# Batch 0's v loads on another engine's queue, and a planner that models GpSimd's load queue

## The chip, the cores and the metric

The kernel runs on one core of a Trainium2 chip. The metric is device time in microseconds (us). A core has five engines that each work through their own instructions in order: TensorE (PE in the profile), VectorE (DVE), ScalarE (ACT), GpSimd (POOL) and SyncE (SP). SP, ACT and POOL can also issue loads and stores, which 16 DMA engines carry out.

## The reference

Attention with a bias by distance, in 8 batches of 8 heads, 576 tokens, 64 channels a head, and behind it a feed-forward layer with a leaky ReLU over all 4608 tokens:

```python
scores = q @ k.T / sqrt(64)
scores = scores + bias_table[bucket(|i - j|)]      # 32 buckets, the last from distance 128 on
attn = softmax(scores)
x = (attn @ v) as [4608, 512]
h = x @ w_in                                       # w_in [512, 2048]
y = max(0.01 * h, h) @ w_out                       # w_out [2048, 512]
```

All inputs and the output are float32; the kernel multiplies in bf16.

## The kernel before

The work of attention is cut into 32 pairs of heads, numbered 0 to 31: four pairs a batch, so pairs 0 to 3 are batch 0, 4 to 7 batch 1, and 8 is the first of batch 2. For a pair, VectorE copies the q and k rows (`rows`, L383), TensorE turns them (`turn_by_pe`, L393), the turned q and k go to `qt` and `kt` (L405), and `apart` (L409) makes the copies for the odd last 64 tokens. TensorE computes the scores in six units u0 to u5 (`score`, L430 to L438), ScalarE takes the exponential of each (`expo`, L444 to L451), VectorE multiplies in the bias near the diagonal (`band`, L463), TensorE multiplies with v in two halves (`av`, L478 and L480), VectorE normalises (L489, L490), and the result is turned into `xT` (L504, L508, or by a DMA). For batch 0 the second half of `av` has a buffer of its own, called ps_om. Scores of pair n are kept in one of two buffers; pair 2 has a third one, and pair 3 writes the buffer that pair 0 used.

The bias enters as a factor: the table's exponential (`exp_table`, L296) is spread by one matmul to a row u (L300, L303), stored to DRAM (`store_u_row`, L306) and read back as band tables hk and hk4 (`load_hk`, L316, and `load_hk4`, L323), all on SP's queue.

The feed-forward layer works on tiles of 512 tokens: 16 blocks of `ffn_in` (4 matmuls each, L521) with a ReLU on ScalarE (L526), then `ffn_out` (L533), a copy (L538) and a store (L543). The first tile lies within batch 0 and needs both halves of w_in, of which blocks 0 to 7 need the first; `ffn_out` needs w_out.

Loads: q and k of the first pair come by SP and ACT. v of batch 0 comes in float32 by six DMAs (`load_v_raw`, L310 and L312, 1.18 MB) and GpSimd casts it (`cast_v`, L331 and L334). All other loads are issued by GpSimd, which casts them on the way, in one queue. Batch b's rows of q and k are in qn0, kn0 for even b and qn1, kn1 for odd b. A `gate` (L337) is a one-element copy on GpSimd into w_in's tile: it waits for its source, and the load of w_in that writes the same bytes waits for it.

The order of the instructions on every engine is set when the kernel is built. `Plan` holds tasks with an engine, a cost in us, the tasks that they come after, and a rank. `Plan.order` simulates the engines and takes, again and again, the task that can start first; the instructions are then written in that order. The costs are thus guesses that decide the order, and the chip then runs each engine's list in order, whatever the true times are. Where the planner expects TensorE to idle, before the first feed-forward block, it puts filler matmuls (`spin`, L710). For a load, `tail` and `land` say when the planner believes that its data is there.

## Time and profile before

| | us |
|---|---|
| median of 3 runs (405.65 to 408.68) | 407.63 |
| the profiled execution | 407.88 |
| its span, first to last instruction | 406.1 |
| TensorE busy | 377.5 (93%) |
| ScalarE busy | 243.2 (60%) |
| VectorE busy | 203.8 (50%) |
| GpSimd busy | 69.8 (17%) |
| mean granted TensorE clock | 0.971 of 2.4 GHz |

The span is what the trace covers; the timed value is 1.8 us longer. A busy time says what share of the span an engine computed, not whether it set the end: matmuls overlap, and an engine that is busy 60% of the time can still be what another waits for in some stretch. The mean clock lies under 1, so part of the execution ran at the lower level of 1.2 GHz.

### The profile page before, as it was taken

The page shows a single profiled execution, that of the slowest core. Times are in us where ns is not written, and L with a number is a line of the kernel's source. Part 1 is how long each engine was busy: PE and PEld are TensorE (multiplying, and loading weights), DVE is VectorE, ACT ScalarE, POOL GpSimd, SP SyncE. Part 2 cuts the span into 40 slices and gives each one's busy share as a digit, 9 for nine tenths or more (in the row PEclk, how much of TensorE's full clock was granted, in tenths as well). Part 3 has the DMA queues.
Part 4 walks back from the last instruction along what each step waited for, and adds up shares of the span by engine and source line. Part 5 has one row for each costly group of instructions (what it writes and reads, how often), then busy time and mean ns, then how long its engine had stood idle before and what let it go on. Part 6 is the DMA issues. An engine that isn't in the chain of part 4 may idle for free.

```text
span 406.1 us, 8302 instructions
## 1 busy us (share of the span) xinstructions
PE 377.5 (93%) x3388; PEld 191.5 (47%) x3388; DVE 203.8 (50%) x539; ACT 243.2 (60%) x345; POOL 69.8 (17%) x112
## 2 busy tenths in 40 slices
PE   3898906999999999999999999999999999999995
PEld 1355403555454554545555455555555544444442
DVE  3498305887667767668567555555444210101021
ACT  1696912856897697877777777777777233333300
POOL 5492613101500700420160040000000000000000
PEclk8699975999999999999999999999999999999999
DMA  9759999833995994898399399111111010010112
GB/s 182 171 84 203 181 205 156 108 87 84 130 154 114 121 184 76 104 178 131 84 149 186 80 105 90 44 44 44 43 44 44 27 46 31 32 47 26 53 52 77
DMA packets 102741, 40.62 MB, mean 100 GB/s; under 512 B 81704, under 2 KB 97072, under 8 KB 102704
## 3 DMA queue, kind: packets, MB, share of 16 engines
q0 software_dynamic: 48512, 17.47, 39.8%
q1 hardware_dynamic: 49280, 21.15, 25.8%
q10 hardware_dynamic: 4912, 1.48, 1.8%
q8 instruction: 26, 0.43, 0.4%
q14 instruction: 11, 0.09, 0.1%
HBM read 37.69 MB, written 9.45 MB: 116 GB/s over the span
## 4 chain that ended last, share of the span: by engine, by line
PE 84%; DMA 9%; ACTq 2%; POOL 2%; issue 1%; DVE 1%; ACT 1%; POOLq 0%
PE pm L533 31%; PE pm L521 30%; PE ps_o L478 9%; PE ps_s L430 7%; DMA kn<-in_k_dram 4%; DMA v<-in_v_dram 4%; PE ps_o L480 2%; DMA w_in_sb<-in_moe_w_in_dram 2%; PE ps_s L434 1%; PE ps_s L437 1%; ACTq L312 1%; PE ps_t L393 1%; POOL vn L331 1%; ACTq L310 1%; PE ps_w L710 0%
## 5 line engine op out<-in xcount | busy, mean ns | idle before, releaser
L521 PE MATMUL pm<-xT,w_in_sb 128*128 128x512 bf16 x576 | 147.2, 383 | 0.0
L533 PE MATMUL pm<-w_out_sb,gt 128*128 128x512 bf16 x576 | 144.3, 379 | 0.0
L526 ACT ACTIVATE gt<-pm 128x512 bf16<-128x512 f32 x144 | 86.1, 601 | 92.2 <-PE pm L521 90.9
L444 ACT ACTIVATE at<-ps_s 128x1024 bf16<-128x1024 f32 x124 | 120.1, 1024 | 27.0 <-PE ps_s L430 26.4
L533 PEld LDWEIGHTS <-gt 128*128 128x128 bf16 x576 | 52.6, 98 | 67.1 <-issue 10.6
L521 PEld LDWEIGHTS <-w_in_sb 128*128 128x128 bf16 x576 | 52.8, 98 | 63.5 <-issue 6.8
L463 DVE TENSOR_TENSOR at<-at,hk 128x768 bf16<-128x768 bf16 (+3 forms) x155 | 69.4, 461 | 22.1 <-ACT at L444 17.2
L478 PEld LDWEIGHTS <-at 128*128 128x128 bf16 x1240 | 52.7, 98 | 31.0 <-DVE at L463 16.7
L538 DVE COPY y<-pm 128x512 f32<-128x512 f32 x36 | 24.8, 690 | 83.8 <-PE pm L533 83.4
L478 PE MATMUL ps_o<-vn,at 128*128 128x65 bf16 x1180 | 54.0, 195 | 13.6 <-DVE at L463 13.6
L480 PE MATMUL ps_o<-v,at 128*128 128x65 bf16 x295 | 47.9, 195 | 0.2 <-POOL v L334 0.2
L201 POOL DMA_DIRECT2D vn<-in_v_dram x24 | 21.6, 911 | 141.4 <-PE ps_o L480 132.3
L430 PE MATMUL ps_s<-qt,kt 64*128 64x512 bf16 x256 | 40.9, 388 | 1.2 <-ACT at L446 0.5
L489 DVE RECIPROCAL rcp<-ps_o 128x5 f32<-128x5 f32 x60 | 11.7, 194 | 43.5 <-PE ps_o L480 43.1
L490 DVE TENSOR_TENSOR opair<-ps_o,rcp 128x320 bf16<-128x320 f32 x60 | 29.5, 492 | 2.0
L480 PEld LDWEIGHTS <-at 128*128 128x128 bf16 x310 | 30.4, 98 | 0.0
L446 ACT ACTIVATE at<-ps_s 128x512 bf16<-128x512 f32 x31 | 18.6, 601 | 11.4 <-PE ps_s L434 11.3
L405 DVE COPY qt<-tu 128x576 bf16<-128x576 bf16 x22 | 14.8, 670 | 14.1 <-PE ps_s L438 14.1
L451 ACT ACTIVATE at<-ps_s 128x576 bf16<-128x576 f32 x31 | 20.3, 655 | 0.2 <-PE ps_s L438 0.2
L383 DVE COPY pr<-qn 96x768 bf16<-96x768 bf16 x31 | 11.1, 358 | 15.2 <-DMA qn<-in_q_dram 15.2
L430 PEld LDWEIGHTS <-kt 64*128 64x128 bf16 x256 | 8.5, 94 | 21.5 <-issue 18.7
L405 DVE COPY kt<-tu 128x576 bf16<-128x576 bf16 x22 | 14.7, 667 | 0.0
(77 smaller groups left out, 202.2 us busy)
## 6 DMA issues: line engine op xcount, KB each, us to landing
out_dram<-y SPq DMA_DIRECT2D x36, 256.0 KB, 2.0
qn<-in_q_dram POOLq DMA_DIRECT2D x14, 288.0 KB, 9.9
kn<-in_k_dram POOLq DMA_DIRECT2D x14, 288.0 KB, 10.7
vn<-in_v_dram POOLq DMA_DIRECT2D x28, 128.0 KB, 6.0
w_in_sb<-in_moe_w_in_dram POOLq DMA_DIRECT2D x2, 1024.0 KB, 11.6
w_out_sb<-in_moe_w_out_dram POOLq DMA_DIRECT2D x2, 1024.0 KB, 13.9
first<-in_v_dram ACTq DMA_DIRECT2D x4, 256.0 KB, 8.7
hk<-u_row SPq DMA_DIRECT2D x1, 576.0 KB, 6.2
```

The costliest lines, as they stand in the source:

```text
L201: nc.gpsimd.dma_start(out=vn[i][:, c, :, 0:D], in_=v[b, :, c * P : (c + 1) * P, :].rearrange("h s d -> s h d"),)
L405: copy(out=t[:, 0:S].rearrange("p (r c) -> p r c", c=NC), in_=src)
L430: nc.tensor.matmul(ps[:, e, :], lhsT=kt[r, u * P : (u + 1) * P], rhs=qt[r, 0:512], start=True, stop=True)
L444: nc.scalar.activation(at[:, :, u, 0:512], ps, AF.Exp, scale=scale)
L463: nc.vector.tensor_tensor(out=o, in0=o, in1=m, op=ALU.mult)
L478: nc.tensor.matmul(ps[:, ic, :], lhsT=at[:, o : o + P], rhs=vn[i][:, c, 2 * p + e, :], start=(c == 0), stop=False)
L480: nc.tensor.matmul(ps[:, ic, :], lhsT=at4[:, ic * P : (ic + 1) * P], rhs=v4[i][:, p, e, :], start=False, stop=True)
L490: nc.vector.tensor_tensor(out=opairs[n][:, :, e * D : (e + 1) * D], in0=ps[:, :, 0:D], in1=rcp.to_broadcast([P, NJ + 1, D]), op=ALU.mult)
L521: nc.tensor.matmul(pm[:, j * w : (j + 1) * w], lhsT=w_in_sb[:, c, f * P : (f + 1) * P], rhs=xT[c][:, t0 : t0 + w], start=(c == 0), stop=(c ...
L526: nc.scalar.activation(gts[T][:, f0 : f0 + TT // w, 0:w], pms.pop((T, f0)).rearrange("p (j t) -> p j t", t=w), AF.Prelu, bias=0.0, scale=1 ...
L533: nc.tensor.matmul(ys[T, ts], lhsT=gts[T][:, f, ts * P : (ts + 1) * P], rhs=w_out_sb[:, f, :], start=(f == 0), stop=(f == n_fc - 1))
L538: nc.vector.tensor_copy(out=y, in_=ys[T, ts])
```

## The change

It does four things. The six v loads of batch 0 are issued by SP, as a task that comes after the store of the u row, and whose rank puts it behind the band loads. The planner gets a model of GpSimd's load queue: each load has a time `moves`, and `ring` makes each load's data come after that of the load before; the numbers for `land` and `tail` go. The gate of w_in's first half waits for the last v load in place of hk, and the casts of v stand behind that load's issue. And v of batch 1 is loaded before the second half of w_in. Some costs and due times are set anew.

```diff
@@ -59,7 +59,7 @@
 
     def order(self):
 
-        free, done, waiting = {}, [], {}
+        free, done, waiting, ring = {}, [], {}, 0.0
         for t in self.tasks:
             waiting.setdefault(t["engine"], []).append(t)
         first = False
@@ -90,7 +90,9 @@
             _, t, r = best
             e = t["engine"]
             waiting[e].remove(t)
-            t["start"], t["end"] = r, max(r + t["cost"] + t["tail"], t.get("land", 0.0))
+            t["start"], t["end"] = r, r + t["cost"] + t["tail"]
+            if "moves" in t:
+                t["end"] = ring = max(ring, r + t["cost"] + 2.0) + t["moves"]
             t["idle"] = r - free.get(e, 0.0)
             free[e] = r + t["cost"]
             for k in t["take"]:
@@ -307,9 +309,9 @@
 
     def load_v_raw():
         for c in range(NJ):
-            nc.scalar.dma_start(out=vraw_sb[:, c, :, :], in_=v[0, :, c * P : (c + 1) * P, :].rearrange("h s d -> s h d"))
+            nc.sync.dma_start(out=vraw_sb[:, c, :, :], in_=v[0, :, c * P : (c + 1) * P, :].rearrange("h s d -> s h d"))
         for e in range(2):
-            nc.scalar.dma_start(out=vraw4[e * SL : (e + 1) * SL, :, :],
+            nc.sync.dma_start(out=vraw4[e * SL : (e + 1) * SL, :, :],
                                 in_=v[0, e::2, NJ * P : S, :].rearrange("h s d -> s h d"))
 
     def load_hk(h0, h1):
@@ -333,8 +335,8 @@
         for e in range(2):
             nc.gpsimd.tensor_copy(out=v4[0][e * SL : (e + 1) * SL, :, e, 0:D], in_=vraw4[e * SL : (e + 1) * SL, :, :])
 
-    def gate(t):
-        nc.gpsimd.tensor_copy(out=w_in_sb[0:1, 0, 0:1], in_=t)
+    def gate(t, row=0):
+        nc.gpsimd.tensor_copy(out=w_in_sb[row : row + 1, 0, 0:1], in_=t)
 
     def mirrored(t, lo, hi):
 
@@ -550,37 +552,39 @@
     def dma(at):
         return add("DMA0", 0.0, [], None, 0, at=at)
 
-    L["raw", 0], L["raw", 1], tabl = dma(3.6), dma(3.8), dma(3.4)
+    L["raw", 0], L["raw", 1], tabl = dma(4.0), dma(4.2), dma(3.8)
     sh = add("DVE", 0.1, [tabl], shift_table, -1)
     e8t = add("ACT", 0.25, [sh], exp_table, -1)
     spr = add("PE", 0.4, [e8t], spread_table, -1, take=["O"])
     cpu = add("DVE", 0.6, [spr], copy_u_row, -1, give=["O"])
-    urt = add("SP", 0.1, [cpu], store_u_row, -1, tail=2.6)
-    hkt = add("SP", 0.1, [urt], lambda: load_hk(0, 2), -1, tail=2.8)
+    urt = add("SP", 0.1, [cpu], store_u_row, -1, tail=2.8)
+    hkt = add("SP", 0.1, [urt], lambda: load_hk(0, 2), -1, tail=3.2)
     hkr = add("SP", 0.1, [urt], lambda: (load_hk(2, H), load_hk4()), 1, tail=5.5)
+    vrt = add("SP", 0.5, [urt], load_v_raw, 2, tail=6.0)
+    vrt["land"] = 18.0
     L["hk", 0], L["hk", 1] = hkt, hkr
 
     prev = []
 
-    def pool_load(key, cost, go, after=(), land=0.0):
-        t = add("POOL", cost, prev + list(after), go, 1, tail=2.5)
-        t["land"] = land
+    def pool_load(key, cost, go, moves, after=(), rank=1):
+        t = add("POOL", cost, prev + list(after), go, rank)
+        t["moves"] = moves
         prev[:] = [t]
         L[key] = t
-
+        return t
+
+    QK, VB, WH = 3.9, 9.5, 5.6
     L["qk", 0, 0], L["qk", 0, 1] = dma(7.0), dma(9.5)
-    pool_load(("qk", 0, 2), 1.6, lambda: (gate(ub[0:1, 0:1]), load_qk(0, 6, H)), after=[cpu], land=17.0)
-    vrt = add("ACT", 0.6, [], load_v_raw, 5, tail=9.0)
-    vc = [add("POOL", 0.7, [vrt], lambda c=c: cast_v(c), 0) for c in range(NJ + 1)]
+    pool_load(("qk", 0, 2), 1.6, lambda: (gate(ub[0:1, 0:1]), load_qk(0, 6, H)), QK / 2, after=[cpu])
+    pool_load(("w_in", 0), 1.0, lambda: (gate(vraw4[SL : SL + 1, 0, 0:1], SL), load_w_in(0)), WH, after=[vrt])
+    vc = [add("POOL", 0.6, [vrt] + prev, lambda c=c: cast_v(c), 0) for c in range(NJ + 1)]
     vt[0] = vc[-1]
-    pool_load(("w_in", 0), 0.8, lambda: (gate(hk[0:1, H - 1, 0:1]), load_w_in(0)), after=[hkr], land=22.0)
-    pool_load(("qk", 1, 0), 1.6, lambda: load_qk(1, 0, 4), land=26.0)
-    pool_load(("w_in", 1), 0.8, lambda: load_w_in(1), land=32.0)
-    pool_load(("v", 1), 5.5, lambda: load_v(1, 0, H, False), land=42.0)
-    vt[1] = L["v", 1]
-    pool_load(("qk", 1, 1), 1.6, lambda: load_qk(1, 4, H), land=46.0)
-    pool_load(("w_out", 0), 0.9, lambda: load_w_out(0), land=52.0)
-    pool_load(("w_out", 1), 0.9, lambda: load_w_out(1), land=58.0)
+    pool_load(("qk", 1, 0), 1.6, lambda: load_qk(1, 0, 4), QK)
+    vt[1] = pool_load(("v", 1), 5.5, lambda: load_v(1, 0, H, False), VB)
+    pool_load(("w_in", 1), 0.8, lambda: load_w_in(1), WH)
+    pool_load(("qk", 1, 1), 1.6, lambda: load_qk(1, 4, H), QK)
+    pool_load(("w_out", 0), 0.9, lambda: load_w_out(0), WH)
+    pool_load(("w_out", 1), 0.9, lambda: load_w_out(1), WH)
 
     def plan_rows(n):
         b, p = items[n]
...
@@ -667,11 +671,9 @@
         i = n_pairs * (b - 2)
         for hh in range(2):
             ps = [rowt[i + 2 * hh + x][r] for x in range(2) for r in range(2)]
-            L["qk", b, hh] = add("POOL", 1.5, ps + prev, lambda hh=hh: load_qk(b, 4 * hh, 4 * hh + 4), 10 * i + 500, tail=11.0)
-            prev[:] = [L["qk", b, hh]]
+            pool_load(("qk", b, hh), 1.5, lambda hh=hh: load_qk(b, 4 * hh, 4 * hh + 4), QK, ps, 10 * i + 500)
         avs = [t for p in range(n_pairs) for t in avt[i + p]]
-        vt[b] = add("POOL", 5.0, avs + prev, lambda: [load_v_part(b, j) for j in range(3)], 10 * i + 500, tail=11.0)
-        prev[:] = [vt[b]]
+        vt[b] = pool_load(("v", b), 5.0, lambda: [load_v_part(b, j) for j in range(3)], VB, avs, 10 * i + 500)
 
     yts, oin, ins = [], {}, {}
 
```

On ScalarE, from its start: `e_171` is the exponential of the bias table, `first` the tile that receives raw q, k and v. Before:

```order
L256 DMA first<-in_k_dram 96x2x384
L261 ACT_TABLE_LOAD
L261 ACTIVATE warm<-warm 128x1
L310 DMA first<-in_v_dram 128x8x64 x4
L312 DMA first<-in_v_dram 64x4x64 x2
L296 ACTIVATE e_171<-tab 32x8
L383 CAST pr<-first 96x768
L405 COPY qt<-ps_t 128x576
```

And now:

```order
L258 DMA first<-in_k_dram 96x2x384
L263 ACT_TABLE_LOAD
L263 ACTIVATE warm<-warm 128x1
L298 ACTIVATE e_171<-tab 32x8
L385 CAST pr<-first 96x768
L407 COPY qt<-ps_t 128x576
```

The two rows of v loads (six DMAs) are gone from ahead of the exponential.

On GpSimd, behind the row of u (`qn_102`, `kn_104`, `vn_106` and `v_1_108` belong to batch 1, `vn_105` and `v_0_107` to batch 0). Before:

```order
L409 TENSOR_TENSOR kt_111<-kt_111,own 128x128
L409 TENSOR_TENSOR qt<-qt,own 128x128
L331 CAST vn_105<-first 128x8x64
L334 CAST v_0_107<-first 64x4x64 x2
L337 COPY w_in_sb<-hk 1x1
L349 DMA w_in_sb<-in_moe_w_in_dram 128x4x1024
L193 DMA qn_102<-in_q_dram 96x4x384
L193 DMA kn_104<-in_k_dram 96x4x384
L349 DMA w_in_sb<-in_moe_w_in_dram 128x4x1024
L223 DMA vn_106<-in_v_dram 128x8x64 x4
L228 DMA v_1_108<-in_v_dram 64x4x64 x2
L193 DMA qn_102<-in_q_dram 96x4x384
```

And now:

```order
L411 TENSOR_TENSOR qt<-qt,own 128x128
L411 TENSOR_TENSOR kt_111<-kt_111,own 128x128
L339 CAST w_in_sb<-first 1x1
L351 DMA w_in_sb<-in_moe_w_in_dram 128x4x1024
L333 CAST vn_105<-first 128x8x64 x4
L336 CAST v_0_107<-first 64x4x64 x2
L195 DMA qn_102<-in_q_dram 96x4x384
L195 DMA kn_104<-in_k_dram 96x4x384
L225 DMA vn_106<-in_v_dram 128x8x64 x4
L230 DMA v_1_108<-in_v_dram 64x4x64 x2
L351 DMA w_in_sb<-in_moe_w_in_dram 128x4x1024
L195 DMA qn_102<-in_q_dram 96x4x384
```

The gate (1x1 into w_in_sb) and w_in's first half moved ahead of the casts of v, all casts stand together behind them, and w_in's second half moved behind v of batch 1.

On VectorE, in batch 1: `at1_114` with hk are the band multiplies of pair 4 (and with at0_113 of pair 5), `qn0_101` and `kn0_103` are here rows of batch 2 (pairs 8 and 9), `qn1_102` and `kn1_104` the rows of pair 6. Before:

```order
L409 TENSOR_TENSOR qt_788<-qt_788,own_112 128x128
L383 COPY pr_821<-qn0_101 96x768
L383 COPY pr_821<-kn0_103 96x768
L383 COPY pr_833<-qn0_101 96x768
L383 COPY pr_833<-kn0_103 96x768
L463 TENSOR_TENSOR at1_114<-at1_114,hk_99 128x2x320
L463 TENSOR_TENSOR at4_1_116<-at4_1_116,hk4_100 128x192
L489 RECIPROCAL rcp_892<-ps_o_859 128x5
L490 TENSOR_TENSOR opair_891<-ps_o_859,rcp_892 128x5x64
L463 TENSOR_TENSOR at0_113<-at0_113,hk_99 128x2x256
L463 TENSOR_TENSOR at0_113<-at0_113,hk_99 128x2x384
L383 COPY pr_931<-qn1_102 96x768
```

And now:

```order
L407 COPY kt2_111<-ps_t_778 128x576
L411 TENSOR_TENSOR kt2_111<-kt2_111,own_112 128x128
L411 TENSOR_TENSOR qt_786<-qt_786,own_112 128x128
L465 TENSOR_TENSOR at1_114<-at1_114,hk_99 128x2x384
L465 TENSOR_TENSOR at1_114<-at1_114,hk_99 128x2x320
L465 TENSOR_TENSOR at4_1_116<-at4_1_116,hk4_100 128x192
L491 RECIPROCAL rcp_892<-ps_o_858 128x5
L492 TENSOR_TENSOR opair_891<-ps_o_858,rcp_892 128x5x64
L385 COPY pr_927<-qn1_102 96x768
L385 COPY pr_927<-kn1_104 96x768
```

The copies from qn0 and kn0 no longer stand ahead of the last two band multiplies of pair 4, and the copies of pair 6 come before them.

On SP, the six v loads now stand between the band loads and the first turns and stores of later stages.

## Rows read from the trace of the kernel before

**Rows 1.** Busy time by stretch: us from the start, length, busy us (instructions) by engine, clock, DMA
```profile
41.20:50.60 9.40, 9.40 (x73) 4.33 (x71) 3.61 (x8) 8.83 (x14) 6.26 (x9) 1.00 1.68 183
64.20:68.00 3.80, 3.80 (x20) 1.81 (x21) 2.25 (x7) 0.60 (x1) 1.50 (x2) 0.50 2.31 145
68.00:406.10 338.10, 333.89 (x2935) 168.28 (x2932) 168.70 (x433) 207.51 (x296) 36.54 (x48) 1.00 0.58 86
```
**Rows 2.** What TensorE waited for: us in total, times, longest
```profile
PE ps_o L478 <- DVE at L463: 13.6, 1, 13.6
PE ps_u L300 <- ACT e L296: 6.8, 1, 6.8
PE ps_w L710 <- DVE junk L246: 1.2, 1, 1.2
```
**Rows 3.** Timeline of VectorE: start us, us, line, tiles, idle before and its releaser
```profile
36.56 0.36 DVE L383 COPY pr<-kn 96x768 bf16<-96x768 bf16 x1 [0.95 <-DMA kn<-in_k_dram]
...
46.11 0.22 DVE L409 TENSOR_TENSOR qt<-qt,own 128x128 bf16<-128x128 bf16 x1
61.41 0.61 DVE L383 COPY pr<-qn 96x768 bf16<-96x768 bf16 x1 [15.08 <-DMA qn<-in_q_dram]
```
**Rows 4.** Line L193, 40 to 45 us: k of batch 1's second half, issue and landing
```profile
L193 POOL DMA_DIRECT2D kn<-in_k_dram x1: 669/669/669, 41.8 to 41.8; - x1
...
DMA to landing us min/median/max: 8.0/8.0/8.0
```
**Rows 5.** Line L193, 45 to 50 us: q and k of batch 2, issues and landings
```profile
L193 POOL DMA_DIRECT2D qn<-in_q_dram x2: 669/680/690, 46.1 to 48.1; - x2
...
L193 POOL DMA_DIRECT2D kn<-in_k_dram x2: 672/672/673, 47.5 to 48.8; - x2
...
  DMA v<-in_v_dram: 0.7, 1
...
DMA to landing us min/median/max: 15.3/15.7/16.9
```
**Rows 6.** Timeline of all engines in the first 16 us
```profile
6.50 4.95 ACTq L312 DMA_DIRECT2D first<-in_v_dram  x2
...
6.88 0.15 DVE L293 TENSOR_TENSOR tab<-tab 32x8 f32<-32x8 f32 x1 [2.95 <-DMA tab<-in_bias_table_dram]
...
11.49 0.21 ACT L296 ACTIVATE e<-tab 32x8 bf16<-32x8 f32 x1 [8.78 <-issue]
...
13.08 0.33 SPq L306 DMA_DIRECT2D u_row<-ub  x1
...
15.27 1.02 ACT L444 ACTIVATE at<-ps_s 128x1024 bf16<-128x1024 f32 x1 [1.67 <-PE ps_s L430]
```
**Rows 7.** Line L323, the last two band loads on SP: issues and landings
```profile
L323 SPq DMA_DIRECT2D hk<-u_row x2: 605/649/693, 15.3 to 16.1; - x2
...
DMA to landing us min/median/max: 5.7/5.9/6.1
```
**Rows 8.** Line L312, the last two v loads on ACT: issues and landings
```profile
L312 ACTq DMA_DIRECT2D first<-in_v_dram x2: 619/2454/4290, 6.5 to 10.8; - x2
...
DMA to landing us min/median/max: 2.7/4.8/6.9
```
**Rows 9.** Busy time by stretch, at the end of the v loads; the last number is GB/s
```profile
9.50:11.50 2.00, 0.00 (x0) 0.00 (x0) 0.00 (x0) 0.01 (x1) 0.00 (x0) 0.50 1.21 249
```
**Rows 10.** Timeline of GpSimd, 18 to 25 us: casts of v, gate, w_in's first half
```profile
18.52 1.72 POOL L331 CAST vn<-first 128x512 bf16<-128x512 f32 x3
...
22.33 1.37 POOL L334 CAST v<-first 64x256 bf16<-64x256 f32 x2
23.76 0.39 POOL L337 COPY w_in_sb<-hk 1x1 bf16<-1x1 bf16 x1
24.45 0.81 POOL L349 DMA_DIRECT2D w_in_sb<-in_moe_w_in_dram  x1 [0.30 <-POOL w_in_sb L337]
```
**Rows 11.** Timeline of ScalarE, 26 to 37 us: pair 2, and the end of pair 3
```profile
26.37 3.82 ACT L444 ACTIVATE extra<-ps_s 128x1024 bf16<-128x1024 f32 x4
...
35.98 0.65 ACT L451 ACTIVATE at<-ps_s 128x576 bf16<-128x576 f32 x1 [0.24 <-PE ps_s L438]
```
**Rows 12.** Timeline of TensorE: the first two blocks of `ffn_in`
```profile
41.74 1.90 PE L521 MATMUL pm<-xT,w_in_sb 128*128 128x512 bf16 x8
```
**Rows 13.** Line L349, the two halves of w_in: landing after issue
```profile
L349 POOL DMA_DIRECT2D w_in_sb<-in_moe_w_in_dram x2: 757/785/813, 24.4 to 26.6; - x2
...
DMA to landing us min/median/max: 8.3/11.6/14.9
```

More of the change, by code (lines that the diff above doesn't have):

```diff
@@ L613, in plan_rows @@
                  lambda: take_turned(n, 1, nc.scalar.copy if n == n_pairs else nc.vector.tensor_copy), feed, give=give)
-        on, cost = ("POOL", 0.35) if n in (1, 2) else ("DVE", 0.2)
+        on, cost = ("POOL", 0.5) if n in (1, 2) else ("DVE", 0.2)
         ak = add(on, cost, [ck], lambda: apart(n, kts[n]), feed + 1)
```

## The prediction

> **What bounds the kernel now.** I read the busy time in stretches first. TensorE computes without a pause from 68.0 us to its last matmul: 333.89 us busy of 338.10, and the 4.2 us left are the last copy and store [rows 1]. So the end is set by when this unbroken run begins, and by how much of TensorE's work is still to be done then. The list of its waits says what delayed the run: one wait of 13.6 us for a VectorE multiply at L463, one of 6.8 us for the exponential of the bias table, and nothing else above 1.2 us [rows 2]. Next the timeline of VectorE over the long wait: it finished at 46.3 us and then stood for 15.08 us in front of a `rows` copy, whose data came at 61.4 us [rows 3]. The question is which load that was. The second half of batch 1 (its k half was issued at 41.8 us) landed 8.0 us later, at 49.8 us [rows 4]. The pairs of loads of batch 2, of which the first q part was issued at 46.1 us, took 15.3 to 16.9 us, so it came at 61.4 [rows 5]. VectorE stood for batch 2, and behind that copy were queued the last two band multiplies of pair 4, which TensorE wanted, and the copies of pair 6, whose data had been there for 11 us. The order of VectorE shows the same: the copies from qn0 stand ahead of the band multiplies and of the copies from qn1. After the wait TensorE ran at half its clock (0.50, which is 1.2 GHz) from 64.2 to 68.0 us [rows 1].
>
> **The start.** The bias table was in place when VectorE used it at 6.88 us, but ScalarE made its exponential only at 11.49, after 8.78 us in which it issued loads; the last two v loads alone held its queue from 6.50 to 11.45 [rows 6]. The row of u is stored at 13.08, and the first exponential of scores starts at 15.27 [rows 6].
>
> **Part 1: v off ScalarE's queue.** The chain is table, exponential, TensorE, u row. Without the v loads the exponential waits for the table alone. If the table lands as before, e8 starts at 6.88 + 0.15 + 0.06 = 7.1 us; it may land earlier, since the v loads share the DMA engines with it, but VectorE needs the table and has other copies until 3.93 (6.88 less 2.95, [rows 6]), so e8 cannot start before 4.2. I take 5.7, the middle, as no row shows the table's load alone. That is 5.8 us earlier (4.4 to 7.3). The first score exponential moves with it, to 9.5 us (10.9 at the late end; at the early end k's raw load holds it to about 9.1), and the u row's store to 7.3 (5.8 to 8.7).
>
> **What it costs: v comes later.** On SP the v loads stand behind four band loads, of which the last two are issued from u store + 2.3 to + 3.6 and have landed by + 8.7 (16.1 + 5.7 = 21.8 against 13.08) [rows 6, 7]. Then v's 1.18 MB need 4.7 us at the 249 GB/s that the DMA engines moved when v was nearly alone [rows 9]: v is in at store + 13.4 = 20.7 us. Bounds: store + 9.3 if it overlaps the band loads fully (six issues of 0.6 us [rows 8] and a landing of 2.7), so 15.1; and store + 15.8 if the six loads take the 12.2 us (1.3 to 10.8 + 2.7 = 13.5 [rows 8]) that they took on ScalarE's queue, so 24.5. Queued behind the new wait on GpSimd are the first half of w_in, the casts of v and every load of batch 1. The casts ended at 23.7 before; now they end at v + 1.5 (gate to end of the w_in issue, 23.76 to 25.26) + 3.7 (three in 1.72, one more 0.6, the last two 1.37) [rows 10] = v + 5.2 = 25.9 us.
>
> Who waits for that: pair 3 writes the buffer that pair 0's product with v reads, and TensorE's new order puts that product after the third score unit of pair 2. ScalarE reaches this point 13.97 us after its first exponential (26.37 + 3 x 0.955 - 15.27) [rows 6, 11], at 23.5; the product is done some 0.35 later (only its last parts need the last cast), so ScalarE loses about 3 us there. From that point 7.4 us of exponentials remain (36.63 - 29.24) [rows 11], and 0.4 restarts the chain: the last exponential of batch 0 ends at v + 13.3 = 34.0 us. The bounds are 30.5 (v in time, no wait; 9.1 + 21.4) and 37.8 (v at 24.5). Before, it ended at 36.63 and the unbroken stretch began at 41.20, 4.57 us later [rows 1, 11], of which 0.95 was VectorE waiting for k of pair 4 [rows 3]. I take 4.1, so the stretch begins at 38.1 us: **3.1 us gained** (7.1 at best, 1.2 lost at worst).
>
> The Trainium skill speaks against this part: "DMA: Bandwidth & Descriptors", section "Issuing engines are not separate DMA queues", says that loads issued from several engines run on the same 16 DMA engines, and that another issuer saves only issue time, usually small. Here the rows disagree on small: 8.78 us of issue [rows 6] lie on the path. By the rule taken whole the 3.1 us would be about none; that is the first rival.
>
> **Part 2: the planner and the loads of batch 1.** In the new order of VectorE the copies from qn1 (pair 6) stand behind all bands of pair 4, and no copy from qn0 precedes them. So the 13.6 us vanish if each load of the new sequence is there when TensorE wants it. The loads move the same bytes; from the issue of w_in's first half (24.45 [rows 10]) to the landing of k of pairs 6 and 7 (49.8 [rows 4]) it was 25.4 us, w_in's first half took 8.3 and the second landed at 26.6 + 14.9 = 41.5 [rows 13]. With v in at 20.7 the issue is at 21.5, so pairs 6 and 7 land at 46.9. The second half of w_in changes places with v of batch 1, so it should land when that v did: by 47.5, when the k load that waited for it was issued [rows 5], 23.0 us after 24.45, so now by 44.5. TensorE reaches the ninth block of `ffn_in`, the first that needs it, after 8 blocks of some 0.9 us (two took 1.90, [rows 12]) and some 2.2 us of score and turn work, at 47.5; it turns pair 6 at 49.5. That leaves margins of 3 us each. No wait replaces the 13.6, and without the pause the half clock goes too: 3.8 us at half rate cost 1.9. I add 1 us (0 to 4) for short gaps, since ScalarE was busy 8.83 of 9.40 us in the dense stretch [rows 1].
>
> **Sum** against this execution: 406.1 - 3.1 - 13.6 - 1.9 + 1.0 = 388.5 us of span. 407.88 was timed, 1.8 above the span and 0.25 above the median of 407.63; so 388.5 + 1.8 - 0.25 = **390.0 us**. Bounds: 385.0 (7.1, 13.6, 1.9, no gaps) and 397 (1.2 lost, 4 of gaps).
>
> **Rivals.** (a) The start gives nothing: v takes the 12.2 us on SP that it took on ScalarE. Issued at store + 3.6 = 10.9 it is in at 23.1, the last exponential of the batch ends at 36.4 and the stretch begins at 40.5 to 41: 393. For it: the same bytes on the same engines. Against: the raw q and k loads are over by then. The page of the Trainium skill named above would lead here. (b) A load of batch 1 still comes late: casts of v now stand between w_in's issue and q and k of batch 1, and VectorE in order would stop on pair 6 with TensorE behind it. If those lands slip by 9 us against the 3 us of margin, 6 us are lost: 396. Against: w_in's first half takes 8.3 us [rows 13], and the next load is issued 5 us into it. (c) Slower than before: GpSimd stands at the gate, in order, with all of batch 1 behind it. Each us that v is later than 17 us moves everything by one; the gain of 17.6 us is gone from v at 38 us, and at 43 the time is 412. That needs 32 us from issue to landing where ScalarE's queue shows 12.2. (d) The order does not do what it says, and VectorE waits 10 us or more at another copy that precedes ready work: 403.
>
> **How the numbers follow.** The forecast with its bounds 385 to 394 gets 0.68, (a) 0.14, (b) 0.10, (c) 0.03, (d) 0.05. About 1 per cent is what a measurement of this kernel can tell (its three runs span 0.7 per cent). Faster by over 1 per cent (below 403.5) are the forecast, (a), (b) and a little of (d): 0.93; the same 0.04; slower 0.03. For 8 in 10 the range goes from 384.5 to 397.
>
> **What would show it.** Right: e8's wait of 8.78 us gone and the first score exponential near 9.5; the gate at 20 us and w_in issued behind it; TensorE's wait for L463 gone, no half clock after 60 us, an unbroken run from 38 us. Wrong: a TensorE wait above 3 us at the ninth block of `ffn_in` or at pair 6's turn, v landing past 25 us, or a table that is not there at 7 us.

## The result, and the profile after

The changed kernel takes 393.93 us (median of 4 runs, 393.79 to 394.38) against 407.24 before (the three runs of above and a fourth): a ratio of 0.968, 95% interval 0.964 to 0.971. The prediction was 390.0, with a range from 384.5 to 397. Its profiled execution has a span of 392.2 us (406.1 before), so 13.9 us are to be explained. The sum forecast 17.6: 3.1 from the start, 13.6 and 1.9 from batch 1, less 1.0 for gaps.

First the list of TensorE's waits in the changed kernel (us in total, times, longest); it answers to [rows 2]. All line numbers are now two higher.

```profile
PE ps_o L480 <- POOL vn L333: 4.5, 4, 3.5
PE ps_u L302 <- ACT e L298: 1.4, 1, 1.4
PE ps_w L712 <- DVE junk L248: 1.2, 1, 1.2
PE pm L523 <- ACT gt L528: 1.0, 1, 1.0
```

The 13.6 us of [rows 2] are gone, and the exponential of the table holds TensorE for 1.4 us in place of 6.8. A new line stands on top: pair 0's product with v waits 4.5 us for the casts of v. After 42 us the longest wait is the 1.0 us at L523.

Next the timeline of VectorE where it takes up pair 6, as in [rows 3].

```profile
51.34 0.80 DVE L465 TENSOR_TENSOR at<-at,hk 128x640 bf16<-128x640 bf16 x2 [2.35 <-ACT at L448]
...
53.94 0.20 DVE L491 RECIPROCAL rcp<-ps_o 128x5 f32<-128x5 f32 x1 [1.80 <-PE ps_o L482]
...
54.58 0.35 DVE L385 COPY pr<-qn 96x768 bf16<-96x768 bf16 x1
54.84 0.35 DVE L385 COPY pr<-kn 96x768 bf16<-96x768 bf16 x1
```

Pair 4's last band multiplies come first, and the copies of pair 6 follow with no idle time in front (no bracket): their data was there. VectorE stands only for work of TensorE and ScalarE.

The start, from the timelines of all engines; it answers to [rows 6, 10, 11].

```profile
6.05 0.21 ACT L298 ACTIVATE e<-tab 32x8 bf16<-32x8 f32 x1 [3.36 <-DVE tab L295]
...
7.43 0.32 SPq L308 DMA_DIRECT2D u_row<-ub  x1
...
8.97 1.02 ACT L446 ACTIVATE at<-ps_s 128x1024 bf16<-128x1024 f32 x1 [1.19 <-PE ps_s L432]
...
11.10 6.84 SPq L312 DMA_DIRECT2D first<-in_v_dram  x4
...
17.47 0.26 DVE L465 TENSOR_TENSOR at<-at,hk 128x192 bf16<-128x192 bf16 x1 [1.43 <-DMA hk<-u_row]
...
17.98 1.99 SPq L314 DMA_DIRECT2D first<-in_v_dram  x2
...
22.77 0.18 POOL L339 CAST w_in_sb<-first 1x1 bf16<-1x1 f32 x1 [8.01 <-DMA first<-in_v_dram]
...
24.11 2.28 POOL L333 CAST vn<-first 128x512 bf16<-128x512 f32 x4
26.32 0.86 POOL L336 CAST v<-first 64x256 bf16<-64x256 f32 x2
...
28.68 1.02 ACT L446 ACTIVATE extra<-ps_s 128x1024 bf16<-128x1024 f32 x1 [6.00 <-PE ps_s L432]
...
37.32 0.65 ACT L453 ACTIVATE at<-ps_s 128x576 bf16<-128x576 f32 x1
```

The front of the chain came as forecast: the exponential of the table at 6.05 us (forecast 5.7), u's store at 7.43 (7.3), the first exponential of scores at 8.97 (9.5; 15.27 before). But the gate on v opened at 22.77, some 2 us behind the forecast 20.7. ScalarE then stood 6.00 us inside pair 2, and the last exponential of batch 0 ended at 37.97 (forecast 34.0; 36.63 before). The first block of `ffn_in` starts at 41.74 us, exactly as before [rows 12].

Last the busy time by stretch, in the columns of [rows 1] (TensorE's matmuls, its weight loads, VectorE, ScalarE, GpSimd, then the granted clock, the DMA engines' busy share and GB/s): TensorE's idle time for v, what came after it, and 42 to 68 us.

```profile
21.30:24.80 3.50, 0.03 (x1) 0.04 (x2) 0.89 (x2) 1.37 (x2) 1.68 (x4) 1.00 0.09 7
24.90:31.60 6.70, 5.53 (x79) 4.60 (x78) 2.22 (x6) 1.62 (x2) 6.64 (x11) 0.50 1.07 180
...
42.00:68.00 26.00, 24.45 (x253) 12.89 (x252) 15.48 (x41) 22.63 (x34) 8.16 (x11) 1.00 1.52 191
```

TensorE did next to nothing for 3.5 us, and then ran for 6.7 us at a granted clock of 0.50 (1.2 GHz). From 42 to 68 us it is busy for all but 1.55 us, at full clock. That gives the sum as it came out: 406.1 - 0 (start) - 13.6 (wait) - 1.9 (half clock of [rows 1]) + 1.6 (gaps) = 392.2 us. So one thing is to be explained: the part in batch 1 paid in full, less the gaps, and the 6 us that the front of the chain gained had all been lost again by 41.74 us.

### The profile page after: what moved, and what is told of

It reads as the page before. It is cut to its first block, busy times and chain, and to the rows that moved or that the text cites. A ratio compares the mean times of both kernels' runs of the same rounds, so it can differ in the third digit from the quotient of the medians.

```text
span 392.2 us, 8305 instructions
## 1 busy us (share of the span) xinstructions
PE 376.5 (96%) x3388; PEld 191.6 (49%) x3388; DVE 202.8 (52%) x539; ACT 243.6 (62%) x345; POOL 68.8 (18%) x112
## 3 DMA queue, kind: packets, MB, share of 16 engines
q0 software_dynamic: 48512, 17.47, 40.8%
## 4 chain that ended last, share of the span: by engine, by line
PE 89%; SPq 3%; DVE 2%; DMA 2%; ACT 1%; POOL 1%; issue 0%; DVEq 0%; POOLq 0%
PE pm L535 32%; PE pm L523 32%; PE ps_o L480 10%; PE ps_s L432 8%; PE ps_o L482 2%; SPq L312 2%; PE ps_s L436 2%; PE ps_s L439 2%; DMA tab<-in_bias_table_dram 1%; DMA first<-in_v_dram 1%; ACT at L446 1%; DVE opair L492 1%; POOL vn L333 1%; DVE at L465 1%; PE ps_t L395 0%; PE ps_om L480 0%
## 5 line engine op out<-in xcount | busy, mean ns | idle before, releaser
L523 PE MATMUL pm<-xT,w_in_sb 128*128 128x512 bf16 x576 | 145.0, 379 | 1.5 <-ACT gt L528 1.0
L523 PEld LDWEIGHTS <-w_in_sb 128*128 128x128 bf16 x576 | 52.5, 98 | 64.2 <-issue 6.9
L465 DVE TENSOR_TENSOR at<-at,hk 128x768 bf16<-128x768 bf16 (+3 forms) x155 | 68.0, 453 | 24.5 <-ACT at L446 14.6
L480 PEld LDWEIGHTS <-at 128*128 128x128 bf16 x1240 | 53.4, 99 | 22.2 <-issue 8.9
L482 PEld LDWEIGHTS <-at 128*128 128x128 bf16 x310 | 30.7, 99 | 0.5 <-issue 0.5
L436 PEld LDWEIGHTS <-kt 128*128 128x128 bf16 x128 | 9.7, 99 | 6.9 <-ACT at L446 0.5
```

Of the source, the lines that this page charges most:

```text
L465: nc.vector.tensor_tensor(out=o, in0=o, in1=m, op=ALU.mult)
L480: nc.tensor.matmul(ps[:, ic, :], lhsT=at[:, o : o + P], rhs=vn[i][:, c, 2 * p + e, :], start=(c == 0), stop=False)
L482: nc.tensor.matmul(ps[:, ic, :], lhsT=at4[:, ic * P : (ic + 1) * P], rhs=v4[i][:, p, e, :], start=False, stop=True)
L523: nc.tensor.matmul(pm[:, j * w : (j + 1) * w], lhsT=w_in_sb[:, c, f * P : (f + 1) * P], rhs=xT[c][:, t0 : t0 + w], start=(c == 0), stop=(c ...
```

## The experiments

Each diff is against the changed kernel. In every expectation theory A is the part of my theory that the run tests, and theory B its rival. My theory after the result: (A) the gain of 13.9 us is the order of batch 1's work, and the gain of the start is eaten by v's late landing and by what TensorE and ScalarE do while they wait for it. Its rivals: moving v did contribute and something else ate it; the DMA engines are the bound, whoever issues; ScalarE or the planner's order is the bound at the start. This table has the main readings of each run in us (profiled execution; the median is of 4 to 6 runs). "v in" is the start of the first GpSimd instruction that waits for all of v. The ratio is to runs of the kernel before on the same chip as the run. The runs come from several chips: the four from "planner alone" on share one, the four from "a third of v" on another, and the last three share one with the second row of the changed kernel. That kernel itself differs by 0.4 us between two chips, and the kernel before by up to 0.7, so smaller differences across such groups are not read.

| kernel | v in | pair 0's product starts | `ffn_in` starts | span | median | ratio to before, 95% |
|---|---|---|---|---|---|---|
| before | - | 22.50 | 41.74 | 406.1 | 407.24 | |
| changed | 22.77 | 24.77 | 41.74 | 392.2 | 393.93 | 0.964 to 0.971 |
| changed, with the last four | 22.46 | 24.46 | 41.58 | 392.0 | 393.53 | 0.967 to 0.969 |
| planner alone | - | 22.63 | 40.60 | 391.2 | 392.91 | 0.961 to 0.969 |
| v's move alone | 22.94 | 24.94 | 39.79 | 401.1 | 403.38 | 0.989 to 0.995 |
| idle matmuls | 22.80 | 24.81 | 39.25 | 389.7 | 391.71 | 0.959 to 0.968 |
| v from two queues | 22.41 | 24.80 | 40.70 | 391.1 | 393.38 | 0.963 to 0.971 |
| a third of v | 18.82 | 21.87 | 37.65 | 387.8 | 389.84 | 0.957 to 0.963 |
| casts shared, first try | 23.38 | 33.84 | 45.16 | 395.1 | 395.85 | 0.972 to 0.976 |
| v by GpSimd | 22.29 | 26.05 | 37.52 | 388.4 | 389.86 | 0.957 to 0.960 |
| v told later | 22.29 | 27.66 | 39.29 | 390.1 | 391.68 | 0.961 to 0.968 |
| casts shared, second try | 22.52 | 24.75 | 35.51 | 389.3 | 390.93 | 0.960 to 0.963 |
| v by GpSimd, told earlier | 22.03 | 22.35 | 38.71 | 391.1 | 393.24 | 0.965 to 0.970 |
| w_in ahead of v again | 22.61 | 24.82 | 40.73 | 391.4 | 393.81 | 0.967 to 0.970 |

One regularity of the table helps with all that follows. The span less the start of `ffn_in` is 349.9 to 350.9 us in ten of the thirteen profiles with the planner's model or with v's move, and 364.4 in the kernel before. It is longer in three: v's move alone (361.3), the second try at sharing the casts (353.8) and v told earlier (352.4). So the planner's gain lies behind the start of `ffn_in`, and what brings that start forward comes on top of it, save in the three.

### The planner alone

```
-            nc.sync.dma_start(out=vraw_sb[:, c, :, :], in_=...
+            nc.scalar.dma_start(out=vraw_sb[:, c, :, :], in_=...
...
-    vrt = add("SP", 0.5, [urt], load_v_raw, 2, tail=6.0)
+    vrt = add("ACT", 0.6, [], load_v_raw, 5, tail=9.0)
...
+    pool_load(("w_in", 0), 0.8, lambda: (gate(hk[0:1, H - 1, 0:1]), load_w_in(0)), WH, after=[hkr])
```

> The planner's ring model and the new order of batch 1's loads alone; v of batch 0 stays on ScalarE's queue, and the casts stand ahead of w_in as before the change. Theory A (moving v gained nothing: v landed 1.9 us later than forecast and ffn_in began at 41.74 us in both kernels, so the whole gain is the order of batch 1): the wait of 13.6 us for pair 4's band multiply is gone, the unbroken stretch begins near 41.2 us, and the time is that of the changed kernel, 392 to 395 us. Theory B (moving v gained some 3 us that something else in the changed kernel ate): the time is 397 us or more.

392.91 us: theory A. The exponential of the table is as late as ever in its timeline, and TensorE waits for it as in [rows 2]:

```profile
11.15 0.21 ACT L298 ACTIVATE e<-tab 32x8 bf16<-32x8 f32 x1 [8.44 <-issue]
```

```profile
PE ps_u L302 <- ACT e L298: 6.7, 1, 6.7
```

Yet the wait of 13.6 us is gone and the kernel is no slower than the changed one. `ffn_in` starts at 40.60 us here, about 1 us earlier than in the changed kernel. Moving v, taken on top of the planner, gains nothing (392.91 against 393.53 and 393.93 for the changed kernel; the intervals overlap and the chips differ, so I do not claim a loss).

### The move of v alone

```
-            t["start"], t["end"] = r, r + t["cost"] + t["tail"]
-            if "moves" in t:
-                t["end"] = ring = max(ring, r + t["cost"] + 2.0) + t["moves"]
+            t["start"], t["end"] = r, max(r + t["cost"] + t["tail"], t.get("land", 0.0))
...
+    pool_load(("w_in", 1), 0.8, lambda: load_w_in(1), land=32.0)
+    pool_load(("v", 1), 5.5, lambda: load_v(1, 0, H, False), land=42.0)
```

> The move of v alone: v on SP's queue, the gate on v, w_in ahead of the casts, and the planner and the load order of before. In its order VectorE has the copies of batch 2's q and k ahead of the last bands of pair 5. Theory A: the move by itself gains nothing in the dense stretch and VectorE still stands for batch 2's q, which lands some 37 us after w_in's issue (61.4 less 24.45 before), so near 60 us, a stall of about 10 us or more at pair 5; time 400 to 408 us. Theory B (the move of v is what ended the stall, by shifting the loads): no wait of TensorE above 4 us after 45 us, and a time near the changed kernel's 394 us.

403.38 us: theory A; the stall is a little shorter than I expected, and it stands not at pair 5, as I wrote, but still at pair 4: between the first half of its product with v (which ends at 52.6 us) and the second. A line of TensorE's waits, and VectorE's timeline:

```profile
PE ps_o L478 <- DVE opair L490: 8.8, 1, 8.8
```

```profile
50.74 0.35 DVE L383 COPY pr<-kn 96x768 bf16<-96x768 bf16 x1
60.02 0.63 DVE L383 COPY pr<-qn 96x768 bf16<-96x768 bf16 x1 [8.94 <-DMA qn<-in_q_dram]
```

Behind the copies of pair 6, which are now done in time, VectorE again stands for batch 2's q, and the normalization of that first half, which TensorE needs before the second, is queued behind that. So the planner's model, not the earlier start, removes the stall. One thing did not fit A: here `ffn_in` starts at 39.79 us, 2 us earlier than before. With the old planner the same move of v did win 2 us at the start. That pointed to the new planner's order, which a later run takes up.

### Idle matmuls ahead of pair 0's product

```
-            avs.append(add("PE", 0.78, done, lambda e=e: av(n, e), soon + 4, take=[k]))
+            avs.append(add("PE", 0.78, done, lambda e=e: (spin(16) if n + e == 0 else None, av(n, e)), soon + 4, take=[k]))
```

> The changed kernel with 16 idle matmuls just ahead of pair 0's product with v, so that TensorE has work while it waits for v, whose lateness left it idle from 21.3 to 24.8 us and then at a clock of 0.50 from 24.9 to 31.6 us. Theory A (the half clock after that idle time is what stretched the way from v to the last exponential of batch 0 from the forecast 13.3 us to 15.4): the clock stays higher between 25 and 31 us, the last exponential ends 1 to 2 us before 37.97, and the time is near 392 us. Theory B (ScalarE and the order of work bound that stretch, not the clock): the same 394 us within 0.5 us, the clock whatever it is.

391.71 us in the median, 1.8 to 2.2 below the changed kernel: theory A (one of the four runs took 393.69, so the times alone would not settle it; the trace does). The stretch after v, and ScalarE's last exponential of batch 0:

```profile
24.90:31.60 6.70, 5.45 (x117) 4.22 (x117) 3.55 (x11) 3.15 (x4) 6.64 (x11) 1.00 1.07 180
```

```profile
35.22 0.65 ACT L453 ACTIVATE at<-ps_s 128x576 bf16<-128x576 f32 x1
```

In the same 6.7 us TensorE is busy as long as in the changed kernel, but at clock 1.00 it gets 117 matmul records done and not 79. The gate opens at 22.80 us (22.77 without the idle matmuls) and the order is otherwise the same, so only the clock differs, and the batch's exponentials end at 35.87 in place of 37.97. The half clock cost 2.1 us there and 2.5 at the start of `ffn_in`.

### v from two queues

```
+    for c in range(2):
+        nc.scalar.dma_start(out=vraw_sb[:, c, :, :], in_=v[0, :, c * P : (c + 1) * P, :].rearrange("h s d -> s h d"))
...
-        for c in range(NJ):
+        for c in range(2, NJ):
```

> The changed kernel with the first two of the six v loads issued on ScalarE before the bias table's exponential (the first two took 0.4 to 0.6 us each to issue there before the change), the other four on SP as now. Theory A (v's landing at 22.7 us ate the gain of the start, and it is late for the bytes and descriptors that SP's queue has to move behind the band loads): the gate opens at 20 to 21 us, ffn_in begins 1.5 to 3 us before 41.74, time 390.5 to 392.5 us. Theory B (the DMA engines are the limit at the start, whoever issues): the table or k and q come later by what v comes earlier, and the time is 394 us or above. If the table comes 1 us later and the gate 2 us earlier, the two cancel: 393 us.

393.38 us, in neither range (390.5 to 392.5, and 394 or more) and where the expectation has the two cancel. v is in at 22.41, only 0.36 us earlier. The cause is that of theory B. The exponential of the table moves from 6.05 to 7.13 us, the first exponential of scores from 8.97 to 10.90. The DMA engines show why. Here are the stretches from 7 to 10 us of the kernel before, of the changed kernel and of this one, in that order (the last two columns are DMA share and GB/s), and behind them the changed kernel from 16 to 21 us.

```profile
7.00:10.00 3.00, 0.00 (x0) 0.00 (x0) 0.51 (x2) 0.00 (x0) 0.00 (x0) 0.66 1.28 207
```

```profile
7.00:10.00 3.00, 2.96 (x26) 1.31 (x24) 2.17 (x6) 1.67 (x3) 1.50 (x4) 0.64 0.54 63
```

```profile
7.00:10.00 3.00, 2.61 (x16) 1.31 (x16) 2.13 (x5) 1.57 (x3) 1.25 (x3) 1.00 1.11 176
```

```profile
16.00:21.00 5.00, 3.66 (x20) 1.46 (x19) 3.54 (x10) 5.00 (x8) 0.00 (x0) 1.00 0.96 186
```

In the changed kernel v stands behind the band loads on SP, these behind u's row, and the DMA engines are nearly idle meanwhile: 63 GB/s where the kernel before moved 207. The missing 3 x 144 GB/s = 0.43 MB are a third of v; if they come at the end instead, at the 186 GB/s of 16 to 21 us, they take 2.3 us (an estimate). Two early loads fill the hole, but the table's exponential comes 1.1 us and the first scores 1.9 us later, u's row is stored at 8.71 in place of 7.43, and the band loads with the other four v loads move back with it. So a filled hole alone was not shown to bring v in sooner. `ffn_in` starts 1.0 us earlier all the same, and this goes with a clock that is at 0.50 for a shorter time (0.75 in mean from 24.9 to 31.6 us).

### A third of v

```
-        for c in range(NJ):
+        for c in range(1):
...
-            nc.gpsimd.tensor_copy(out=vn[0][:, c, :, 0:D], in_=vraw_sb[:, c, :, :])
+            nc.gpsimd.tensor_copy(out=vn[0][:, c, :, 0:D], in_=vraw_sb[:, 0, :, :])
```

> The changed kernel with three of the four 256 KB loads of batch 0's v left out; the casts of all four parts read the one that is loaded, so batch 0's output is not the reference's, and every instruction but those three loads stays in its place. Theory A (v's landing is what took the gain of the start): v lands near 17 us in place of 22.7, TensorE's wait for the casts shrinks or goes, pair 3 follows as before the change, so the last exponential of batch 0 ends at 31 to 34 us (37.97 now) and the time is 387 to 390 us. Theory B (the last exponential of batch 0 is bound by ScalarE, the bands or the planner's order, and v only seems late): 392.5 us or more.

389.84 us: theory A. GpSimd's gate, the first block of `ffn_in` on TensorE, and the stretch that ran at 0.50 in the changed kernel:

```profile
18.82 0.18 POOL L339 CAST w_in_sb<-first 1x1 bf16<-1x1 f32 x1 [2.61 <-DMA first<-in_v_dram]
...
37.65 1.03 PE L523 MATMUL pm<-xT,w_in_sb 128*128 128x512 bf16 x4
```

```profile
24.90:31.60 6.70, 6.70 (x133) 5.18 (x130) 4.79 (x14) 4.51 (x6) 6.28 (x9) 0.85 1.41 174
```

With every instruction but three loads in place, v is in 3.95 us earlier and `ffn_in` starts 4.09 us earlier. So v's landing is what holds the start here. That is not a rule of one for one, for the clock is part of the 4.09 us: it is 0.85 in mean in this stretch, not 0.50. I expected v near 17 and got 18.8; the 0.79 MB left out are 4.2 us at 186 GB/s, which is near the 3.95 us.

### v told later

```
-    vrt = add("SP", 0.5, [urt], load_v_raw, 2, tail=6.0)
+    vrt = add("SP", 0.5, [urt], load_v_raw, 2, tail=14.0)
```

> The changed kernel with one number of the planner changed: it takes v of batch 0 to land 8 us later (about 22.5 us, as the trace shows). In its order TensorE has all score units of pair 2, and 18 idle matmuls, ahead of pair 0's product with v; the loads and casts are the same. Theory A (v's lateness cost more than v itself, because the planner's order put pair 0's product ahead of pair 2's last scores and ScalarE stood 6.00 us behind it): ScalarE finishes pair 2 near 24.7 us (32.8 now), the clock does not fall, the last exponential ends 2 to 4 us before 37.97 and the time is 390 to 392 us. Theory B (v's landing and the casts alone set the start, the order does not): 393.5 to 394.5 us.

391.68 us: theory A, with no change to any load or cast (one of the four runs took 394.38, so here too the trace says more than the times). The reason is in the code of the change. Not all numbers for `land` went, as I wrote of the change: the line `vrt["land"] = 18.0` is still there, but the new `order` no longer reads `land`; the planner has v in at 16.0 us and puts pair 0's product ahead of pair 2's last three score units. The old planner took the 18.0 (the run with v's move alone), and held back one unit only. Told a time near the true one (24.0 in its count; v is in at 22.29), the planner has ScalarE finish pair 2 first, and the clock stays at 1.00. ScalarE's timeline:

```profile
23.97 0.65 ACT L453 ACTIVATE extra<-ps_s 128x576 bf16<-128x576 f32 x1
29.71 1.94 ACT L446 ACTIVATE at<-ps_s 128x1024 bf16<-128x1024 f32 x2 [5.09 <-PE ps_s L432]
```

Pair 2 ends at 24.62 us (32.82 in the changed kernel). Some gain is thrown away: the 18 idle matmuls that the planner adds run to 27.8, past the last cast at 27.0. These idle matmuls also keep TensorE busy through its wait, so this run does not separate the order from the clock: 16 of them in the changed kernel's own order gave the same 391.7 us.

### The casts shared out, twice

The first try, with the planner told 8 us later:

```
+            copy = (nc.vector.tensor_copy, nc.vector.tensor_copy, nc.scalar.copy, nc.gpsimd.tensor_copy)[c]
...
+    vc = [add(("DVE", "DVE", "ACT", "POOL", "POOL")[c], 0.6, [vrt] + prev, lambda c=c: cast_v(c), 0) for c in range(NJ + 1)]
+    vt[0] = add("PE", 0.0, vc, lambda: None, 0)
```

> The changed kernel with two changes at v of batch 0: the planner is told that it lands 8 us later than it assumed (near the 22.7 us that the trace shows), and its casts are shared out: two parts on VectorE, one on ScalarE, one and the two tails on GpSimd behind w_in. Theory A (from v's landing on the casts in a row on GpSimd, 4.4 us behind the gate, and the order that holds back pair 2's last scores cost what the start had won): the casts end near 25.5 in place of 27.18 us, the last exponential 3 to 5 us before 37.97, and the time is 388 to 391 us. Theory B (after v's landing TensorE's own work on the four pairs sets the start of ffn_in, so neither matters): 393 to 394.5 us.

395.85 us, outside both. The casts do end at 26.9 us, but on TensorE's timeline stand 42 idle matmuls in a row, until 33.8:

```profile
24.78 9.23 PE L713 MATMUL ps_w<-junk 128*128 128x512 bf16 x42
```

The planner filled an idle time that its own model had too long: with `prev`, this edit's casts on VectorE and ScalarE count as coming after the landing of w_in, for which nothing on the chip waits there. TensorE is in order, so pair 0's product starts only at 33.84. This run therefore says nothing on the casts. The second try leaves six of them, and casts ahead of w_in's gate:

```
+            (nc.gpsimd if c < 2 else nc.vector).tensor_copy(out=vn[0][:, c, :, 0:D], in_=vraw_sb[:, c, :, :])
...
+    vc = [add("POOL" if c < 2 or c == NJ else "DVE", 0.5, [vrt] + prev, lambda c=c: cast_v(c), -1) for c in range(NJ + 1)]
```

> The changed kernel with v of batch 0 cast ahead of w_in's gate, two parts and the tails on GpSimd and two parts on VectorE, and with the planner told that v lands 7.5 us later (near 22 us); only 6 idle matmuls now stand between pair 2's scores and pair 0's product. Theory A (from v's landing at 22.3 to 22.8 us the casts in a row behind w_in's issue, 4.4 us, and the held-back scores of pair 2 are what ate the start's gain): the casts end near 24.7, pair 0's product starts near 25, the first block of ffn_in at 36 to 37.5 us (41.74 now), time 387 to 390 us. Theory B (the 395.85 us of the first shared casts came from the casts on VectorE, which hold the bands, and not from the idle matmuls that the planner put in): 393 us or more.

390.93 us, 2.6 below the changed kernel of the same chip, but outside both ranges (387 to 390, and 393 or more). Up to `ffn_in` it is theory A: pair 0's product starts at 24.75 (25 expected), and `ffn_in` at 35.51, even before the 36 to 37.5 us expected. But of 6.1 us gained by then the span keeps 2.7. The rest goes in gaps around pair 4's product with v, where TensorE waits for ScalarE and VectorE in turn, and then at half clock from 49 to 52 us. Two lines of TensorE's timeline and one stretch:

```profile
46.60 0.93 PE L432 MATMUL ps_s<-qt,kt 64*128 64x512 bf16 x4 [0.80 <-ACT at L448]
...
49.22 0.40 PE L480 MATMUL ps_o<-vn,at 128*128 128x65 bf16 x4 [0.81 <-DVE opair L492]
```

```profile
49.00:50.00 1.00, 0.78 (x15) 0.79 (x16) 0.96 (x3) 0.00 (x0) 0.45 (x2) 0.50 1.25 213
```

Whether that is this order of work or would meet every start as early was not tried; the runs whose `ffn_in` starts at 37.5 to 37.7 us lose nothing there (350.2 and 350.9 us to the end).

### v by GpSimd's casting queue, twice

```
-    vrt = add("SP", 0.5, [urt], load_v_raw, 2, tail=6.0)
...
-    vc = [add("POOL", 0.6, [vrt] + prev, lambda c=c: cast_v(c), 0) for c in range(NJ + 1)]
-    vt[0] = vc[-1]
+    vt[0] = pool_load(("v", 0), 5.5, lambda: load_v(0, 0, H, False), VB)
```

> The changed kernel with batch 0's v loaded as the later batches' is, by GpSimd's queue with the cast on the way, right behind q and k of pair 3; no casts on an engine, and the gate of w_in waits for this v. GpSimd issues six loads (4 of 0.88 and 2 of 0.65 us) from 8.9 to 13.7 us, ahead of its multiplies for pairs 1 and 2. Theory A (an earlier issue in the idle DMA time from 7 to 10 us, and no casts, move the start): v is in by 19 us, pair 0's product starts 4 to 5 us earlier, time 387.5 to 391 us. Theory B (the DMA engines move the same bytes by 21 us whoever issues, and pair 1's multiplies, 3 us later, hold its scores): 392.5 us or more.

389.86 us: theory A's time, and a ratio to before of 0.957 to 0.960, the best of all runs. It is not A's way there: v is in no earlier. GpSimd's timeline, and the DMA engines in the stretch shown above for the changed kernel:

```profile
8.98 3.55 POOL L225 DMA_DIRECT2D vn<-in_v_dram  x4
12.48 1.30 POOL L230 DMA_DIRECT2D v<-in_v_dram  x2
...
22.29 0.40 POOL L339 COPY w_in_sb<-v 1x1 bf16<-1x1 bf16 x1 [5.54 <-DMA v<-in_v_dram]
```

```profile
16.00:21.00 5.00, 3.90 (x26) 1.64 (x25) 4.04 (x10) 5.00 (x8) 0.74 (x2) 1.00 1.95 115
```

Its first load is issued 2.1 us earlier and its last 6 us, and v still lands at about 22.2. SP, ScalarE with SP, and GpSimd bring it in between 22.0 and 23.4 us in all eleven profiles of the table with the whole of v on these queues. From the first issue to the landing the six loads took 11.6 us on SP in the changed kernel, 13.2 here, and 12.2 on ScalarE's queue before, where they began at 1.3 us and were in at 13.5: so they take about as long from each of the three, and v is in late because its loads begin late. This fits the Trainium skill ("DMA: Bandwidth & Descriptors", section "Issuing engines are not separate DMA queues"), which says that loads run on the same set of DMA engines whoever issues them. The run with a third of v shows that bytes count. What this run saves is the casts (they ended 4.4 us behind the gate in the changed kernel) and the clock, which holds 1.00 from 18 to 68 us; and it has ScalarE finish pair 2 first, as in the run with v told later. What each of the three is worth was not separated. Pair 0's product starts only at 26.05, though, behind pair 2. So I told the planner that v comes sooner:

```
-    vt[0] = pool_load(("v", 0), 5.5, lambda: load_v(0, 0, H, False), VB)
+    vt[0] = pool_load(("v", 0), 5.5, lambda: load_v(0, 0, H, False), 5.5)
```

> Batch 0's v by GpSimd's casting queue, as in the run before of that kind, with the planner told that it takes 5.5 us and not 9.5 on that queue, which puts pair 0's product back ahead of pair 2's last score units; that run had v in at 22.3 us, but pair 0's product not before 25.8. Theory A (v's landing is the start's bound, so the product should start when v is there): pair 0's product starts at 22.3 to 23 us, ScalarE's wait of 2.29 us at pair 3 goes, ffn_in starts at 35 to 36 us in place of 37.5, time 387 to 388.5 us. Theory B (ScalarE's 5 us per pair and the order of pairs are the bound there, and the product in between holds pair 2 up as in the changed kernel): 389.5 us or more.

393.24 us: theory B's number, but not its reason. Pair 0's product starts at 22.35 and the batch's last exponential ends at 31.80, the earliest of all. Then the next thing is late. VectorE's timeline (the last line is from much later), two of TensorE's waits, and where the first of the two stands:

```profile
33.15 0.35 DVE L385 COPY pr<-qn 96x768 bf16<-96x768 bf16 x1 [1.45 <-DMA qn<-in_q_dram]
34.68 0.36 DVE L385 COPY pr<-kn 96x768 bf16<-96x768 bf16 x1 [0.65 <-DMA kn<-in_k_dram]
...
95.00 0.64 DVE L407 COPY qt<-tu 128x576 bf16<-128x576 bf16 x1 [4.28 <-DMA tu<-pr]
```

```profile
PE ps_o L480 <- DVE opair L492: 2.8, 1, 2.8
PE ps_t L395 <- DVE pr L385: 1.8, 1, 1.8
```

```profile
96.88 0.30 PE L480 MATMUL ps_o<-vn,at 128*128 128x65 bf16 x4 [2.80 <-DVE opair L492]
```

Pair 4's q, issued at 23.41 behind w_in, lands at 33.1, and VectorE in its order stands for it, with two normalizations behind. TensorE waits 1.8 us for the copy and falls to clock 0.50 from 34 to 37 us, and `ffn_in` starts 1.2 us later than in the run before of this kind. It is the old stall in small: a copy that waits for a load, ahead of work that is ready. But it is only a part of the time: the span is 2.7 us longer than in that run, and 1.5 of these come behind the start of `ffn_in`. There TensorE has no gap at all from 42 to 68 us (26.00 us busy, 24.68 in that run). The other wait, of 2.8 us, stands at 96.88 us, behind a VectorE that stood 4.28 us for a DMA that turns rows (`tu<-pr`), and the clock is 0.74 to 0.77 from 97 to 104 us. Why that DMA came late is open. The six runs spread over 3.5 us, and one profile does not say whether all have this wait.

### The order of the two loads

```
-    vt[1] = pool_load(("v", 1), 5.5, lambda: load_v(1, 0, H, False), VB)
     pool_load(("w_in", 1), 0.8, lambda: load_w_in(1), WH)
+    vt[1] = pool_load(("v", 1), 5.5, lambda: load_v(1, 0, H, False), VB)
```

> The changed kernel with w_in's second half issued ahead of batch 1's v again, as before the change; the planner's model of the queue stays. Theory A (the model alone took the 13.6 us away, by putting the copies of batch 2 behind pair 4's bands; which of the two loads comes first has room on both sides): 393 to 394.5 us, no wait of TensorE above 1.5 us after 42 us. Theory B (the reordered loads are part of the gain: v of batch 1 lands some 3 us later and holds pair 4's product): 396 us or more, with a wait for v of batch 1.

393.81 us: theory A. After 42 us no wait of TensorE is above 1.0. The new order of the loads is worth nothing that can be measured; the planner's change took the stall away.

> The changed kernel itself, unaltered, on the same chip as the three others: 393.5 to 394.5 us by both theories. It is the yardstick for differences of 1 or 2 us.

393.53 us (393.26 to 393.81), the yardstick for the three other runs of that chip.

## Why the prediction was right, and where it was not

**The bound, and part 2: right.** The prediction's reading was that VectorE stood for batch 2 with ready work behind it. The planner alone brings 392.91 us, so all of the 13.6 and 1.9 us come from it; v's move alone leaves a stall of 8.8 us of the same kind. The planner's change does it without the reordered loads; its parts (the model of the queue, its numbers, a few new costs) were not tried singly. The margins held: w_in's second half was issued at 33.16 and took at most 11.0 us, so it was in by 44.2 (forecast 44.5), and pair 6's copies waited for nothing. The gaps were 1.6 us for 1.0.

**The start: the front of the chain right, the gain wrong.** Table, exponential, u's row and first scores came within 0.6 us of the forecast. The step that failed is the landing of v. It was forecast at store + 13.4: the band loads in by store + 8.7, and then 4.7 us for v's 1.18 MB at 249 GB/s. It came at store + 15.3, some 2 us later, and both parts were too short. VectorE has the last band load only at 17.47, which is store + 10.0, and v was in 5.3 us behind that. In the kernel before the bands moved when v was in already; now v's first loads, issued at 11.10, run beside them, and the DMA engines moved 186 GB/s from 16 to 21 us, not 249. So bands and v are not two steps one behind the other. On SP the six loads held the queue from 11.10 to 19.97 and were in 11.6 us after the first issue, close to the 12.2 us of ScalarE's queue that the first rival used. The hole from 7 to 10 us is no part of this miss, for the forecast let v begin only behind it; that v could be in sooner without it is argued, and no run shows it.

The next term, "v + 13.3" to the last exponential, came out as 15.2. At full clock it is 13.1 (v in at 22.8, end at 35.87 with the idle matmuls), so its sum held and its unnamed condition did not: that TensorE keeps its clock while it waits. In the sum two misses cancel at full clock: ScalarE resumes 5.2 us behind v (forecast 5.95), and 7.9 us of pair 2 and 3 are left then (forecast 7.4). The prediction looked for half clock only after 60 us. Together the two misses are 4.0 us at the last exponential (37.97 for 34.0); some 0.9 came back on the way to `ffn_in`, and 3.1 forecast became 0. That the time still lies in the range is owed to part 2 and to bounds that allowed for no gain at the start, not to the start's own term. (Two early ends of its ranges do not follow from the rows: "store + 9.3" comes to 9.9 from its own terms, 3.6 + 3.6 + 2.7, and no row shows the "about 9.1" of the first exponential. Neither enters the sum.)

**The rivals.** The first rival, "the start gives nothing", is what happened, at 393 forecast and 393.9 measured; I had given it 0.14 against 0.68. By its own account v's landing alone would do it. Measured, it is about half v's landing (2.1 us) and half the clock (1.9 us). A late load of batch 1, slower than before, and an order that does not do what it says did not happen. Only in the run that started batch 0's products earliest did q of pair 4 become late, which is the second rival's mechanism.

**What stays open.** Whether v's move costs 0.6 to 1.0 us on top of the planner, and why the earliest start of `ffn_in` (35.51 us) loses 3.4 us after 45 us, is not settled by these runs; nor is how much of the start's loss is the order, apart from the clock.

## What to carry to other kernels

A term of the form "x comes at t, and the rest takes as long as it did" holds only if the engines are in the same state at t: ask what TensorE does while it waits, and at what clock it will go on. When a load is queued behind a chain of dependent transfers, look at the DMA engines' rate during that chain, since a byte that does not move then has to move later (argued; the three runs here that issued loads of v earlier brought it in only 0.4 to 0.7 us earlier). And when a scheduler gets a new model, look for numbers that the old one read and the new one does not: one such number stood unread here, and a value near the true one was worth about 2 us.
